# Batch 1 turned in PSUM with its copies apart from TensorE, and a new order on GpSimd, in a fused attention, Fourier mixing and MLP kernel

## The chip, the cores and the metric

The kernel runs on one core of a Trainium2 chip. The metric is the device time of one execution in microseconds (us); the kernel before took 317.34 us (median of three runs, 317.1 to 317.51). The profiled part of an execution, its span, is about 1.8 us shorter than its device time. Engines: PE is TensorE (PEld its weight loads), DVE is VectorE, ACT is ScalarE, POOL is GpSimd, SP is SyncE.

## The reference, cut to what matters

```python
# attention both ways: x (8, 8, 512, 64) with state (8, 8, 32, 64)
scores = x @ state.T / 8;  xread = softmax(scores) @ state      # 512 rows of a batch
scores2 = state @ x.T / 8; sread = softmax(scores2) @ x         # 32 rows of a batch
x = concatenate([xread, sread])          # as (8, 544, 512), float32
# Fourier mixing and an MLP
u  = x + real(fft(fft(x, axis=1), axis=2))
un = (u - mean(u)) / sqrt(var(u) + 1e-6)
out = u + relu(un @ w_ch1) @ w_ch2       # w_ch1 512x2048, w_ch2 2048x512
```

(The softmax and the types are abridged.) Since relu(s·a) = s·relu(a) for a positive s, the kernel multiplies by 1/sqrt(var + 1e-6), its tile `rstd`, only at the very end of a row. This is why `rstd` of batch 0 isn't urgent.

## The kernel before

Eight batches go through one pipeline. While TensorE works on the MLP of one batch, it also gets steps of the next batch's attention and transform. For batches 0 and 1 this overlap is still being built up, and the change is there. The reads of a batch end in tiles XF, XR (rows of the two halves) and XL (32 low rows). They are *folded*, that is, added and subtracted with their mirror images, into XE and XO and then XQ, which the transform multiplies by tables of cosines and sines (`gp`). The results are G, `yp`, U; then `ub` (U minus its mean), turned to `unT`, and the first layer `ph`.

GpSimd works in the order of these lines (cut to what matters):

```python
def more_loads():
    alternate()
    ...
    load_x(2)                                        # SP: x of batch 2
    state_blocks(2, B, nc.gpsimd.tensor_copy)        # casts of states 2 to 7
    nc.gpsimd.tensor_copy(gate, xs_of[2][:, :, 0])   # second gate: reads all four pieces of x
    for q in range(4):
        nc.gpsimd.dma_start(out=w2[...], in_=w2v[...])   # second weights, 4 x 1 MB
    cast_x(2)

def stats_of(u, name):
    ...
    nc.gpsimd.tensor_tensor(rstd, mv[:, 1:2], epst, op=ALU.add)      # a "root": two instructions,
    nc.gpsimd.tensor_tensor(rstd, rstd, mhalf, op=ALU.pow)           # where the statistics are made
    return mv, rstd

def fold_rows(k, eng=nc.vector):
    eng.tensor_add(Sm[:, k], XF[:, k], XR[:, k])
    eng.tensor_add(XE[:, k, 0:256], Sm[:, k, 0:256], Sm[:, k, 512:256:-1])
    eng.tensor_copy(XE[:, k, 256:257], Sm[:, k, 256:257])
    yield
# in batches 0 and 1, GpSimd folds XL and half 0; VectorE folds half 1 and makes XQ
```

A *gate* is a small copy whose only use is to hold GpSimd, and the transfers that it issues next, until its source has landed.

The order of the steps around batch 1 is written out:

```python
for step in (warmed(t0[:2], 2) + [last_sines, more_loads, load_x3] + warmed(t0[2:4], 2) + [exp_again,
        t0[4], t0[8], W(6), s1[1], W(4), t0[5], s1[0], W(16), t0[7], t0[6], s1[2], L[0], s1[3], ...
        L[4], s1[6], t0[13], L[5], L[6], r1[1], r1[2], L[7], r1[3], L[8], r1[4], r1[5], L[9], L[10], r1[7], ...
```

`t0` are steps of batch 0's transform, `L` of its first layer, `s1` and `r1` the scores and reads of batch 1, `W(n)` are n matmuls that only keep TensorE busy. `r1[1]` is sread (with scalings on VectorE), `r1[2]` the low rows' read xlp with GpSimd's low fold.

The softmax here doesn't subtract the row's maximum and nothing guards it: scores larger than these inputs give would overflow.

## Time and profile before

| | before |
|---|---|
| median of three runs | 317.34 us |
| span of the profiled execution | 316.7 us (its device time: 318.47 us) |
| TensorE busy | 298.8 us |
| TensorE idle in the first 100 us | 12.3 us |
| batch 1's transform waits for XQ, then for sT | 1.64 us, 0.86 us |
| x of batch 2 complete, GpSimd's gate opens | 37.82, 38.11 us |

TensorE is full from about 55 us on, so time can only be won ahead of that. The wait for sT is a wait for room: the `gp` tiles and the turned state and x of batch 2 take turns in three PSUM buffers (pool `psQ` in the code), and the third `gp` needs the one out of which VectorE copies batch 2's sT. The lines of the trace stand in the prediction below.

### The profile page before, as it was taken

The page shows a single profiled execution, that of the slowest core. Times are in us where ns is not written, and L with a number is a line of the kernel's source. Part 1 is how long each engine was busy: PE and PEld are TensorE (multiplying, and loading weights), DVE is VectorE, ACT ScalarE, POOL GpSimd, SP SyncE. Part 2 cuts the span into 40 slices and gives each one's busy share as a digit, 9 for nine tenths or more (in the row PEclk, how much of TensorE's full clock was granted, in tenths as well). Part 3 has the DMA queues.
Part 4 walks back from the last instruction along what each step waited for, and adds up shares of the span by engine and source line. Part 5 has one row for each costly group of instructions (what it writes and reads, how often), then busy time and mean ns, then how long its engine had stood idle before and what let it go on. Part 6 is the DMA issues. An engine that isn't in the chain of part 4 may idle for free.

```text
span 316.7 us, 5957 instructions
## 1 busy us (share of the span) xinstructions
PE 298.8 (94%) x2298; PEld 173.0 (55%) x2330; DVE 186.3 (59%) x445; ACT 138.7 (44%) x269; POOL 73.1 (23%) x166
## 2 busy tenths in 40 slices
PE   5878986999999999999999999999999999999995
PEld 5667975554544555456554554455454544455444
DVE  8797565578596684781917864685659573101112
ACT  6698753564553444234442345244433432343300
POOL 8657693240150021300320024001200031000000
PEclk9999999999999999999999999999999999999999
DMA  7998999244836744249363445731342024302055
GB/s 141 197 192 159 203 163 207 62 99 88 165 67 141 174 102 105 81 83 198 77 93 82 69 116 70 147 85 35 83 86 66 35 67 100 83 35 66 35 132 133
DMA packets 111532, 34.22 MB, mean 108 GB/s; under 512 B 102928, under 2 KB 107280, under 8 KB 111504
## 3 DMA queue, kind: packets, MB, share of 16 engines
q1 hardware_dynamic: 100784, 28.08, 43.2%
q0 software_dynamic: 4224, 4.19, 8.4%
q10 hardware_dynamic: 6496, 1.57, 2.4%
q8 instruction: 18, 0.29, 0.4%
q14 instruction: 10, 0.08, 0.1%
HBM read 22.43 MB, written 14.02 MB: 115 GB/s over the span
## 4 chain that ended last, share of the span: by engine, by line
PE 73%; DMA 11%; DVE 9%; POOL 4%; issue 2%; SPq 1%; ACT 0%; POOLq 0%; DVEq 0%
PE po L733 32%; PE ph L667 29%; DMA xs<-in_x_dram 6%; DMA s_dram<-in_state_dram 5%; PE gp L547 3%; DVE U L517 1%; PE po L725 1%; PE yp L513 1%; PE yp L512 1%; DVE st L315 1%; PE eTp L395 1%; PE xfp L408 1%; POOL w L304 1%; DVE ot L698 1%; PE gp L551 1%
## 5 line engine op out<-in xcount | busy, mean ns | idle before, releaser
L733 PE MATMUL po<-w,hT 128*128 128x512 bf16 x477 | 121.9, 379 | 1.4 <-issue 0.8
L669 ACT ACTIVATE hT<-ph 128x512 bf16<-128x512 f32 x112 | 66.9, 597 | 123.5 <-PE ph L667 123.5
L667 PE MATMUL ph<-unT,w 128*128 128x512 bf16 x436 | 114.0, 379 | 1.1 <-DVE ot L698 0.3
L667 PEld LDWEIGHTS <-w 128*128 128x128 bf16 x576 | 51.2, 98 | 48.6 <-issue 1.0
L733 PEld LDWEIGHTS <-hT 128*128 128x128 bf16 x496 | 47.0, 98 | 44.6
L698 DVE SCALAR_TENSOR_TENSOR ot<-po,rstd,U 128x512 f32<-128x512 f32 (+1 forms) x33 | 24.1, 730 | 52.5 <-PE po L733 41.6
L557 POOL COPY GL<-G 128x128 bf16<-128x128 bf16 x8 | 2.4, 300 | 119.6 <-ACT G L555 119.6
L517 DVE TENSOR_TENSOR U<-yp,XR 128x512 f32<-128x512 f32 x16 | 10.9, 682 | 24.4 <-PE yp L513 24.4
L315 DVE BATCH_NORM_STATS2 st<-U 128x6 f32<-128x512 f32 x32 | 21.8, 682 | 0.1
L320 POOL TENSOR_TENSOR rstd<-rstd,mhalf 128x1 f32<-128x1 f32 x34 | 20.3, 597 | 2.7
L319 POOL TENSOR_TENSOR rstd<-mv,epst 128x1 f32<-128x1 f32 x34 | 6.8, 201 | 60.5 <-DVE mv L317 60.5
L555 ACT CAST G<-gp 128x288 bf16<-128x288 f32 x31 | 12.2, 397 | 13.9 <-PE gp L551 8.4
L753 PE MATMUL warm<-ident 128*128 128x128 bf16 x162 | 13.8, 239 | 3.8 <-POOL ident masks.py:199 3.5
L677 PE MATMUL ph<-unT,w 128*128 128x128 bf16 x256 | 15.9, 219 | 0.2 <-ACT unT L591 0.2
L677 PEld LDWEIGHTS <-w 128*128 128x128 bf16 x256 | 15.0, 98 | 0.5 <-issue 0.3
L547 PEld LDWEIGHTS <-XQ 128*128 128x128 bf16 x96 | 8.7, 98 | 11.3 <-DVE XQ L480 4.1
L753 PEld LDWEIGHTS <-ident 128*128 128x128 bf16 x162 | 12.0, 109 | 4.7 <-POOL ident masks.py:199 3.5
L136 POOL CAST xin<-xs 128x2048 bf16<-128x2048 f32 x7 | 13.3, 1895 | 0.0
L581 DVE TENSOR_SCALAR ub<-U,mv 128x512 bf16<-128x512 f32 x24 | 12.3, 513 | 0.9
L408 PEld LDWEIGHTS <-ET 128*128 128x128 bf16 x80 | 7.0, 98 | 10.0 <-DVE XL L417 2.1
L417 DVE TENSOR_TENSOR XR<-xrp,rs 128x512 bf16<-128x512 f32 x16 | 11.1, 695 | 1.2 <-POOL XR L276 0.6
L679 ACT ACTIVATE hT<-ph 128x512 bf16<-128x512 f32 x16 | 9.6, 597 | 5.1 <-PE ph L677 5.1
(183 smaller groups left out, 355.0 us busy)
## 6 DMA issues: line engine op xcount, KB each, us to landing
xs<-in_x_dram SPq DMA_DIRECT2D x30, 256.0 KB, 4.8
w<-in_moe_w_ch_dram POOLq DMA_DIRECT2D x8, 512.0 KB, 11.7
out_dram<-ot SPq DMA_DIRECT2D x15, 256.0 KB, 3.5
r_dram<-ot SPq DMA_DIRECT2D x14, 256.0 KB, 2.2
out_dram<-r_dram SPq DMA_DIRECT2D x14, 256.0 KB, 3.6
xs<-in_x_dram ACTq DMA_DIRECT2D x2, 256.0 KB, 4.1
l_dram<-ot SPq DMA_DIRECT2D x2, 256.0 KB
r_dram<-ot ACTq DMA_DIRECT2D x2, 256.0 KB
```

What stands on the lines that cost most here:

```text
L136: nc.gpsimd.tensor_copy(t[:, :, 1:513], xs)
L315: nc.vector.bn_stats(st6, u)
L320: nc.gpsimd.tensor_tensor(rstd, rstd, mhalf, op=ALU.pow)
L517: nc.vector.tensor_add(u.rearrange("p (k r) -> p k r", r=2), p.rearrange("p (r k) -> p k r", r=2)[:, 0:u.shape[1] // 2, :], x.rearrange("p ...
L547: nc.tensor.matmul(p[:, 0:NM], lhsT=XQ[:, j, c, :], rhs=tab[c], start=(c == 0), stop=(c == 2 and j != 2))
L581: nc.vector.tensor_scalar(t, in0=ud, scalar1=mv[:, 0:1], scalar2=None, op0=ALU.subtract)
L667: nc.tensor.matmul(ph[:, o:o + n], lhsT=w1[:, c, f * 128:(f + 1) * 128], rhs=un_of[key][:, c, :], start=(c == 0), stop=(c == DC - 1))
L669: nc.scalar.activation(hT[:, per * i:per * i + per, :].rearrange("p a b -> p (a b)"), ph, AF.Relu, scale=-1.0 if key in flipped else 1.0)
L677: nc.tensor.matmul(ph[:, o:o + 128], lhsT=w1[:, c, f * 128:(f + 1) * 128], rhs=un_of[key][:, c, 128 * r:128 * r + 128], start=(c == 0), st ...
L698: nc.vector.scalar_tensor_tensor(ot[:, cols], in0=po_of[i][:, 0:cols.stop - cols.start], scalar=rstd, in1=u[:, cols], op0=ALU.mult, op1=AL ...
L733: nc.tensor.matmul(po_of[i], lhsT=h_of[key][:, f, i * 128:(i + 1) * 128], rhs=w2[:, f, :], start=(f == 0), stop=(f == FC - 1))
L753: nc.tensor.matmul(t[:, 0:128], lhsT=ident, rhs=ident, start=(i == 0), stop=(i == n - 1))
```

## The change

The intent has two halves. On GpSimd, the second weights shall be issued as soon as one piece of batch 2's x is there, and the fold of batch 1 shall come ahead of the roots, which nobody needs yet. On TensorE's side, batch 1's x and state are turned into spare PSUM in one go, and the three copies out of it are apart from the turning, so that TensorE doesn't stand behind each copy; sread and xlp change places. Two more edits are not in the cut below: the last two sines of ScalarE come later (after `t0[2:4]`), and `more_loads` is split, its second half (`last_loads`) following them. `weave` interleaves lists of steps; the two numbers behind a list say over which part of the stretch it is spread. The core of the diff:

```diff
-    nc.gpsimd.tensor_copy(gate, xs_of[0][:, :, 0])
+    nc.gpsimd.tensor_copy(gate[:, 0:1], xs_of[0][:, 3, 0:1])
 ...
-        state_blocks(2, B, nc.gpsimd.tensor_copy)
-        nc.gpsimd.tensor_copy(gate, xs_of[2][:, :, 0])
+        nc.gpsimd.tensor_copy(gate[:, 0:1], xs_of[2][:, 0, 0:1])
         for q in range(4):
             nc.gpsimd.dma_start(out=w2[:, q * 4:(q + 1) * 4, :], in_=w2v[:, q * 4:(q + 1) * 4, :])
+        state_blocks(2, 3, nc.gpsimd.tensor_copy)
         cast_x(2)
 ...
+        if roots is None:
+            root()
+        else:
+            roots.append(root)          # batch 0: called after batch 1's fold
 ...
+        def turn_all():
+            p, t = psF.tile([128, 1024], BF16, name="sTp", tag="c"), psX.tile([128, 2, 1024], BF16, name="xTp", tag="x")
+            ...                         # 16 transposes of x, 4 of the state
+            copies.append(lambda: nc.scalar.copy(sT, ...))
+            copies.append(lambda: nc.scalar.copy(xT[:, 0:2, :], t[:, 0]...))
+            copies.append(lambda: nc.vector.tensor_copy(xT[:, 2:4, :], t[:, 1]...))
 ...
-            t0[4], t0[8], W(6), s1[1], W(4), t0[5], s1[0], W(16), t0[7], t0[6], s1[2], L[0], s1[3], ...
-            ... L[5], L[6], r1[1], r1[2], L[7], ... L[9], L[10], r1[7], lambda: state_ones(2, B)]):
+            t0[4], t0[8], W(6), turns1, t0[5], W(10), t0[7], copies1[0], copies1[1], t0[6], copies1[2], L[0], ...
+            r1[2], t0[13], L[5], r1[1], L[6], ... L[8], r1[7],
+            lambda: state_ones(2, B), lambda: [r() for r in first_roots], L[9], L[10]]):
 ...
-          (scores_next, 0.22, 0.86), ([lambda: load_x(4)], 0.6, 0.6))
+          ([lambda: state_blocks(3, B, nc.gpsimd.tensor_copy)], 0.35, 0.35), (scores_next, 0.26, 0.9), ([lambda: load_x(4)], 0.6, 0.6))
```

More of the change, by code (lines that the diff above doesn't have):

```diff
@@ L291, in more_loads @@
     def more_loads():
-        alternate()
         nc.gpsimd.tensor_copy(gate[:, 0:1], XQs[0][:, 3, 0, 0:1])
@@ L296, in more_loads, with last_loads @@
         nc.gpsimd.memset(stb[:, 2:].rearrange("p b g c -> p (b g c)").bitcast(F32), 0.0)
+    def last_loads():
         for hh in range(1, 4):
@@ L311, in x2, with stats_of @@
         return psX.tile([128, 2, 512], F32, name=name, tag="x")
-    def stats_of(u, name):
+    def stats_of(u, name, roots=None):
         st6 = wk.tile([128, 6], F32, name="st6", tag="st6", bufs=4)
@@ L318, in stats_of, with root @@
         rstd = wk.tile([128, 1], F32, name="rstd", tag=name, bufs=16)
-        nc.gpsimd.tensor_tensor(rstd, mv[:, 1:2], epst, op=ALU.add)
-        nc.gpsimd.tensor_tensor(rstd, rstd, mhalf, op=ALU.pow)
+        def root():
+            nc.gpsimd.tensor_tensor(rstd, mv[:, 1:2], epst, op=ALU.add)
+            nc.gpsimd.tensor_tensor(rstd, rstd, mhalf, op=ALU.pow)
+        if roots is None:
+            root()
+        else:
+            roots.append(root)
         return mv, rstd
+    first_roots = []
     x_by_dma, u_by_dma = 3, 2
@@ L347, in turn_state @@
                 return
-            p = psF.tile([128, 1024], BF16, name="sTp", tag="c") if b == 1 else qt("sTp", BF16)
+            p = qt("sTp", BF16)
             for pr in range(4):
@@ L351, in turn_state @@
                 nc.tensor.transpose(p[:, pr * 128:(pr + 1) * 128], sb[:, g, 4 + 128 * hp:132 + 128 * hp], ident)
-            (nc.scalar.copy if b < 2 else nc.vector.tensor_copy)(sT, p[:, 0:512].rearrange("p (a b) -> p a b", b=128))
+            (nc.scalar.copy if b == 0 else nc.vector.tensor_copy)(sT, p[:, 0:512].rearrange("p (a b) -> p a b", b=128))
         def turn_x(g):
@@ L358, in turn_x @@
                 return
-            p = psF.tile([128, 1024], BF16, name="xTp", tag="c") if b == 1 else qt("xTp", BF16)
+            p = qt("xTp", BF16)
             for si in (0, 1, 3, 2):
@@ L363, in turn_x @@
                     nc.tensor.transpose(p[:, o:o + 128], xin[:, si, 1 + 128 * (2 * g + k):129 + 128 * (2 * g + k)], ident)
-            (nc.vector.tensor_copy if b == 0 or g == (b == 1) else nc.scalar.copy)(
+            (nc.vector.tensor_copy if b == 0 or g == 0 else nc.scalar.copy)(
                 xT[:, 2 * g:2 * g + 2, :], p.rearrange("p (a b) -> p a b", b=S))
+        def turn_all():
+            p, t = psF.tile([128, 1024], BF16, name="sTp", tag="c"), psX.tile([128, 2, 1024], BF16, name="xTp", tag="x")
+            for pr in range(4):
+                for si in (0, 1, 3, 2):
+                    nc.tensor.transpose(t[:, pr // 2, 512 * (pr % 2) + 128 * si:512 * (pr % 2) + 128 * si + 128],
+                                        xin[:, si, 1 + 128 * pr:129 + 128 * pr], ident)
+            for pr in range(4):
+                g, hp = pr // 2, pr % 2
+                nc.tensor.transpose(p[:, pr * 128:(pr + 1) * 128], sb[:, g, 4 + 128 * hp:132 + 128 * hp], ident)
+            copies.append(lambda: nc.scalar.copy(sT, p[:, 0:512].rearrange("p (a b) -> p a b", b=128)))
+            copies.append(lambda: nc.scalar.copy(xT[:, 0:2, :], t[:, 0].rearrange("p (a b) -> p a b", b=S)))
+            copies.append(lambda: nc.vector.tensor_copy(xT[:, 2:4, :], t[:, 1].rearrange("p (a b) -> p a b", b=S)))
+        copies = []
         def scores_t(g):
@@ L487, in attend @@
         if b < 2:
-            first = [turn_state, lambda: turn_x(0), lambda: turn_x(1), lambda: scores_t(0), lambda: scores_t(1),
+            first = [turn_state, lambda: turn_x(0), lambda: turn_x(1)]
+            if b == 1:
+                first = [turn_all] + [lambda i=i: copies[i]() for i in range(3)]
+            first += [lambda: scores_t(0), lambda: scores_t(1),
                      lambda: scores(0), lambda: scores(1)]
@@ L572, in centre @@
             u = U[k][:, r, r:r + 512]
-            mv, rstds[k, r] = stats_of(u, "rstd")
+            mv, rstds[k, r] = stats_of(u, "rstd", first_roots if b == 0 else None)
             t = ub[k, r] = wk.tile([128, 512], BF16, name="ub", tag="ub", bufs=5)
@@ L767 @@
     W = lambda n: (lambda: warm(n))
-    for step in (warmed(t0[:2], 2) + [last_sines, more_loads, load_x3] + warmed(t0[2:4], 2) + [exp_again,
-            t0[4], t0[8], W(6), s1[1], W(4), t0[5], s1[0], W(16), t0[7], t0[6], s1[2], L[0], s1[3], t0[9], L[1], t0[10], s1[4],
-            L[2], t0[11], t0[12], L[3], s1[5], r1[0], L[4], s1[6], t0[13], L[5], L[6], r1[1],
-            r1[2], L[7], r1[3], L[8], r1[4], r1[5], L[9], L[10], r1[7], lambda: state_ones(2, B)]):
+    turns1, copies1, s1 = s1[0], s1[1:4], s1[4:]
+    for step in (warmed(t0[:2], 2) + [alternate, more_loads] + warmed(t0[2:4], 2) + [last_sines, exp_again, last_loads, load_x3,
+            t0[4], t0[8], W(6), turns1, t0[5], W(10), t0[7], copies1[0], copies1[1], t0[6], copies1[2],
+            L[0], s1[0], t0[9], L[1], t0[10], s1[1], L[2], t0[11], t0[12], L[3], s1[2], r1[0], L[4], s1[3],
+            r1[2], t0[13], L[5], r1[1], L[6], r1[3], L[7], r1[4], r1[5], L[8], r1[7],
+            lambda: state_ones(2, B), lambda: [r() for r in first_roots], L[9], L[10]]):
         step()
     weave((L[11:], 0, 0.25), (t1, 0.2, 1), ([M[i] for i in (0, 4, 1, 5, 2, 6, 3, 7, 8, 9)], 0.33, 0.99),
-          (scores_next, 0.22, 0.86), ([lambda: load_x(4)], 0.6, 0.6))
+          ([lambda: state_blocks(3, B, nc.gpsimd.tensor_copy)], 0.35, 0.35), (scores_next, 0.26, 0.9), ([lambda: load_x(4)], 0.6, 0.6))
     l2 = M
```

## The prediction

> **What bounds the kernel now.** I read the page first: how full TensorE is and where it is not.
>
> ```profile
> PE 298.8 (94%) x2298; PEld 173.0 (55%) x2330; DVE 186.3 (59%) x445; ACT 138.7 (44%) x269; POOL 73.1 (23%) x166
> ...
> PE   5878986999999999999999999999999999999995
> ```
>
> TensorE is busy 94% of 316.7 us, and from slice 8 on (each slice is 7.9 us) it is full. Whatever the change does must therefore happen in the first seven slices, some 55 us, and a microsecond won there moves everything behind it. Next, busy time by stretch (columns: length, then busy us of PE, PEld, DVE, ACT, POOL):
>
> ```profile
> 20.00:25.00 5.00, 3.43 (x37) 2.49 (x34) 3.67 (x9) 4.97 (x16) 2.07 (x7) 1.00 1.21 197
> 25.00:30.00 5.00, 4.27 (x64) 3.91 (x65) 3.74 (x8) 4.66 (x8) 4.83 (x12) 1.00 0.65 120
> 30.00:40.00 10.00, 10.00 (x169) 9.60 (x167) 6.49 (x18) 7.22 (x14) 5.39 (x8) 1.00 1.10 210
> 40.00:51.40 11.40, 8.57 (x142) 7.97 (x139) 5.55 (x15) 6.61 (x13) 10.21 (x19) 1.00 1.16 172
> 51.40:55.00 3.60, 2.68 (x23) 1.85 (x25) 3.29 (x15) 0.80 (x2) 0.00 (x0) 1.00 1.23 214
> ```
>
> TensorE lacks 1.57 + 0.73 + 0 + 2.83 + 0.92 = 6.05 us there. While it lacks 2.83 us in the fourth stretch, GpSimd is the full engine (10.21 of 11.40). The list of who waited for whom, TensorE from 25 to 60 us (columns: total, times, longest):
>
> ```profile
> PE gp L547 <- DVE XQ L480: 1.6, 1, 1.6
> PE xfp L408 <- DVE XL L417: 1.1, 1, 1.1
> PE gp L547 <- DVE sT L352: 0.9, 1, 0.9
> PE yp L513 <- ACT G L555: 0.6, 1, 0.6
> PE tp L590 <- ACT ub L579: 0.4, 1, 0.4
> PE ph L677 <- ACT unT L591: 0.2, 1, 0.2
> ```
>
> The largest, batch 1's transform (gp) waiting for XQ, leads to VectorE and from there to GpSimd, as the timelines of both show (start, length, instruction, idle before and its end):
>
> ```profile
> 38.11 0.19 POOL L302 COPY gate<-xs 128x4 f32<-128x4 f32 x1 [2.65 <-DMA xs<-in_x_dram]
> 38.57 3.04 POOL L304 DMA_DIRECT2D w<-in_moe_w_ch_dram  x4 [0.27 <-issue]
> 41.58 1.93 POOL L136 CAST xin<-xs 128x2048 bf16<-128x2048 f32 x1
> 43.41 0.33 POOL L557 COPY GL<-G 128x128 bf16<-128x128 bf16 x1
> ...
> 47.22 0.67 POOL L462 TENSOR_TENSOR XE<-XL 32x256 f32<-32x256 bf16 x1
> ...
> 50.57 0.19 POOL L471 CAST XE<-Sm 128x1 f32<-128x1 bf16 x1
> ```
>
> ```profile
> 50.79 0.56 DVE L480 TENSOR_TENSOR XQ<-XE 128x384 bf16<-128x384 f32 x1 [3.53 <-POOL XE L471]
> ```
>
> VectorE had its own half of the fold by 47.3 us and then stood 3.53 us until GpSimd's half came at 50.76. GpSimd was late because it works in order: it waited for all of batch 2's x (37.8), spent 3.04 us issuing the second weights, 1.93 on a cast, 0.33 on GL, and 3.5 us (43.67 to 47.14) on four pairs of rstd, which nobody needs before the first output at 63.96 us. Only then came the folds, 3.5 us.
>
> **What the Trainium skill says.** "Perfetto Trace Analysis", section "Tensor Engine Instruction (MATMUL, LD_WEIGHTS)": ACT, DVE and GpSimd are strict first in, first out. The trace agrees: folds whose XL was there at 41.4 us stand behind roots until 47.2. "DMA: Bandwidth & Descriptors", section "Queues, rings and completion order": each DMA engine goes round robin between queues, a packet at a time. The trace agrees: packet by packet, the SP queue (256-byte packets) moved 221 KB/us from 29 to 36 us alone, but 40 KB/us from 17 to 25 us beside the first weights, which moved 155. "SBUF — State Buffer", section "SBUF: two separate sides": GpSimd and VectorE share a port pair that one instruction holds whole. The trace fits: VectorE's Sm over 128x514 took 0.66 us beside batch 0's GpSimd fold, 0.43 us in batch 1 where GpSimd did a root.
>
> **The change, part by part.** The built order of both kernels was compared engine by engine.
>
> *First gate.* The copy ahead of the first weights now reads one piece of x. The copy before it ends at 10.1 us, when all of x of batch 0 (last piece 8.3) has landed. Worth 0.
>
> *Second gate and GpSimd's order.* It waits for the second piece of batch 2's x, which landed at 34.04 us (all: 37.82). The weights issue at about 34.4 to 37.5. Then the state casts of batch 2 alone: the four of 768 elements took 3.73 us; I take 1.0 us for 128 elements each, so 38.5. The cast of x, if x is in by then: 40.4. The low fold, 1.45 us (0.67 + 0.14 + 0.63): 41.9. Sm needs XF and XR, which I put at 40.6 below: 43.1; XE 0.8: 43.9. So GpSimd's half comes at about 44 instead of 50.8, ahead of TensorE. Roots move to 44 to 47.5, the casts of the other states later; both are needed only from 60 us on.
>
> *ScalarE's order in the head.* The copy of G (j=2) no longer stands behind two sines (23.89 to 24.66): it starts at 23.9, and the yp that waited 0.55 us is held only by VectorE's G of 24.84. So U starts at 25.28 instead of 25.72, and mv is ready at 26.92. ub no longer waits behind the 1.0 us copy of xT: it starts at 26.95, not 27.78. With the old distances (0.78 to tp, 0.43 to unT, 0.64 to ph) ph starts at 28.75 instead of 29.63. But ScalarE now has unT, sT (0.49) and xT (0.91) in a row: xT is there at 30.0, scores start at 30.05 (before 30.52), TensorE idles 0.4 us, and the next ub comes at 30.65, another 0.2 us. By the xrp of batch 1 (34.90 before) I expect 34.65. Of 0.9 us won, 0.25 stays. The ten warm matmuls fewer (10 at about 56 ns) only fill a wait: 0.
>
> *xlp ahead of sread.* Before, xfp stood 1.06 us behind XL, plus 0.16 once more. Now xlp comes one step of the first layer and one score after xrp, so XL is early (37.4). XF is then behind sread's four scalings (1.17 us) on VectorE: I work out waits of 0.3 before the second xfp and 0.3 before the last xrp. Net 1.2 - 0.6 = 0.6 us. The last xrp now precedes two more steps of the first layer (0.89 us each), so VectorE's fold is done at 43.3, XQ begins at 44 and is complete at 47. TensorE, after seven steps, reaches gp at 48.5 to 48.9 and finds XQ: the 1.64 us fall away.
>
> *sT.* The 0.86 us stood behind VectorE's six XQ passes and eight memsets (50.8 to 54.2). These are now done before TensorE arrives, so the copy follows its transpose: 0.86 us fall away.
>
> Sum: 0.25 + 0.6 + 1.64 + 0.86 = 3.35 us, perhaps 0.3 more from the small waits. Taken: 3.6 us, so 317.34 - 3.6 = 313.7. From 55 us on TensorE is full and does the same work, so the shift is kept.
>
> **Rivals.**
>
> *The second weights hold up x.* Issued at 34.4, their packets start about 1.9 us later (before: 38.57 to 40.46), at 36.3, when batch 2's last small piece and all of batch 3's x are under way. Slowed by 221/40 = 5.5, the remaining 1.5 us would take 8.3: x at 44.6, cast 46.5, folds 50: the 1.64 us stay, and with part of the 0.86 the gain is 1 to 1.5, time about 316. For it: the rates above. Against it: at 36.5 all of the piece before it and six of the small piece's eight writes had landed, and batch 3's last small piece met the start of the same weights and took 1.46 us after its predecessor, against 1.34. XQ has about 4 us to spare.
>
> *VectorE becomes the bound at 60 to 80 us* (16.8 of 20 busy). TensorE lacks only 0.94 us there now, and VectorE's work there hangs on TensorE's own products, so it moves with them. If it eats the gain: 315.5. The changed weave (scores of batch 2 a little later) can move this by 0.5 either way.
>
> *ScalarE's row of copies costs more than it saves.* If the scores wait longer than 0.4 us, up to 0.7 goes: 314.4.
>
> *All idle time goes*: 6.05 us at most, 311.3. The waits inside batch 0's fold (before 23 us) are untouched, so this is unlikely.
>
> **Range and chances.** Between the first rival and the best case, leaning to the sum: 312.4 to 315.6. Two per cent are 6.3 us, more than all idle time in reach: faster 0.04, same 0.95, slower 0.01.
>
> **What would show it.** GpSimd's last XE at 43 to 46 us, ahead of gp. No wait of gp for XQ or sT over 0.3 us. The weights issued at 34.4. A cast of batch 2's x starting by 41; beyond 44 the first rival is right. First ph at 28.7, then a wait of the scores for xT. gp of batch 1 at 48.5 to 49 and, from yp on, all of TensorE's work 3.3 to 3.9 us earlier to the end. Wrong if gp still waits, or if the gain at 55 us is not there at 311.

## The result, and the profile after

The changed kernel took 315.34 us (median of four runs, 315.33 to 315.38) against 317.22 (four runs, 317.09 to 317.51) for the kernel before. The ratio is 0.994, 95% interval 0.9922 to 0.9957. A ratio here is the mean time of one kernel's fast runs over that of the other's of the same rounds, so it isn't quite the ratio of the medians quoted. Executions over 1.5% slower than the fastest of the same kernel are left out of the means. The spans of the two traces are 316.7 and 313.6 us: trace to trace the gain is 3.1 us, timed it is 1.9.

The page of the changed kernel, busy time of each engine and TensorE in 40 slices:

```profile
PE 300.5 (96%) x2320; PEld 172.4 (55%) x2320; DVE 187.0 (60%) x445; ACT 138.5 (44%) x269; POOL 74.8 (24%) x170
...
PE   5878999999999999999999999999999999999995
```

The 8, 7 and 6 in slices 5 to 7 have become 9. Busy time by stretch, as in the prediction (length, then busy us of PE, PEld, DVE, ACT, POOL, granted clock, DMA, GB/s):

```profile
20.00:25.00 5.00, 3.75 (x39) 2.72 (x37) 3.53 (x9) 4.96 (x16) 2.04 (x6) 1.00 1.21 197
25.00:30.00 5.00, 4.03 (x61) 3.48 (x59) 3.17 (x7) 4.12 (x7) 4.86 (x13) 1.00 0.46 80
40.00:51.40 11.40, 11.13 (x168) 9.96 (x166) 7.77 (x23) 7.47 (x17) 10.71 (x18) 1.00 1.19 189
51.40:55.00 3.60, 3.60 (x32) 2.30 (x30) 0.88 (x2) 1.73 (x3) 1.63 (x3) 1.00 1.18 234
```

TensorE now lacks 0.27 us from 40 to 51.4 us, where it lacked 2.83, and nothing from 51.4 to 55, where it lacked 0.92. GpSimd is just as full from 40 to 51.4, and TensorE no longer minds. TensorE's waits from 25 to 60 us (total, times, longest):

```profile
PE ph L706 <- ACT unT L620: 0.7, 1, 0.7
PE eTp L398 <- ACT xT L388: 0.4, 1, 0.4
```

The waits for XQ, sT, XL, G and ub are gone. The wait of the first ph for unT was there before too (0.23 us); that it is 0.67 now I put down to the ten fewer matmuls that do nothing ahead of it, which wasn't tested (ph itself starts at 28.65, earlier than the 29.63 of before). GpSimd's timeline (start, length, instruction, idle before it and what ended that):

```profile
35.17 0.19 POOL L302 COPY gate<-xs 128x1 f32<-128x1 f32 x1 [4.57 <-DMA xs<-in_x_dram]
35.63 3.04 POOL L304 DMA_DIRECT2D w<-in_moe_w_ch_dram  x4 [0.28 <-issue]
...
40.05 1.89 POOL L136 CAST xin<-xs 128x2048 bf16<-128x2048 f32 x1
42.03 0.66 POOL L488 TENSOR_TENSOR XE<-XL 32x256 f32<-32x256 bf16 x1
...
45.68 0.18 POOL L497 CAST XE<-Sm 128x1 f32<-128x1 bf16 x1
45.81 0.19 POOL L322 TENSOR_TENSOR rstd<-mv,epst 128x1 f32<-128x1 f32 x1
```

The fold's last piece ends at 45.86 instead of 50.76, and the roots follow it. VectorE and TensorE then:

```profile
45.90 0.56 DVE L506 TENSOR_TENSOR XQ<-XE 128x384 bf16<-128x384 f32 x1 [0.63 <-POOL XE L497]
```

```profile
48.56 0.41 PE L576 MATMUL gp<-CT,XQ 128*128 128x288 bf16 x2
...
61.60 0.38 PE L619 MATMUL tp<-ident,ub 128*128 128x128 bf16 x4 [0.63 <-ACT ET L422]
```

VectorE now waits 0.63 us for GpSimd instead of 3.53, and XQ is complete at 48.66, hardly ahead of use: `gp` takes its parts one after another from 48.56. Behind it, `yp` starts at 54.10 instead of 58.04. Of these 3.94 us the last line gives some back: at 61.6 us TensorE waits 0.63 us for ScalarE's ET, a wait that the kernel before doesn't have. At the end of the span 3.1 us are left.

### The profile page after: what moved, and what is told of

Same layout as the page of the kernel before. It is cut to its first block, busy times and chain, and to the rows that moved or that the text cites. A ratio compares the mean times of both kernels' runs of the same rounds, so it can differ in the third digit from the quotient of the medians.

```text
span 313.6 us, 5980 instructions
## 1 busy us (share of the span) xinstructions
PE 300.5 (96%) x2320; PEld 172.4 (55%) x2320; DVE 187.0 (60%) x445; ACT 138.5 (44%) x269; POOL 74.8 (24%) x170
## 4 chain that ended last, share of the span: by engine, by line
PE 81%; DVE 12%; ACT 2%; DMA 2%; issue 1%; SPq 0%; DVEq 0%; ACTq 0%
PE po L762 32%; PE ph L696 29%; PE gp L576 3%; PE ph L706 3%; DMA xs<-in_x_dram 2%; DVE U L546 2%; DVE st L316 1%; PE yp L542 1%; PE po L754 1%; PE yp L541 1%; PE xfp L434 1%; PE xrp L434 1%; PE gp L580 1%; PE esp L409 1%; DVE XF L443 1%
## 5 line engine op out<-in xcount | busy, mean ns | idle before, releaser
L762 PE MATMUL po<-w,hT 128*128 128x512 bf16 x496 | 125.0, 379 | 0.0
L782 PE MATMUL warm<-ident 128*128 128x128 bf16 x152 | 12.8, 237 | 3.8 <-POOL ident masks.py:199 3.4
L782 PEld LDWEIGHTS <-ident 128*128 128x128 bf16 x152 | 11.1, 107 | 4.7 <-POOL ident masks.py:199 3.4
```

What stands on the lines that cost most here:

```text
L762: nc.tensor.matmul(po_of[i], lhsT=h_of[key][:, f, i * 128:(i + 1) * 128], rhs=w2[:, f, :], start=(f == 0), stop=(f == FC - 1))
L782: nc.tensor.matmul(t[:, 0:128], lhsT=ident, rhs=ident, start=(i == 0), stop=(i == n - 1))
```

## The experiments

All ran on one chip and gave correct results. The runs of the kernel before: 318.43 us (316.55 to 319.61, 11 runs), 316.65 (316.37 to 316.93, 7 runs). The second call has 318.44 (12 runs), but 11 of these are those of the first, so the ratios of e5 to e8 rest on runs of the kernel before from another call. Already these medians tell something: the kernel before moves over 3.2 us, the changed one stays within 315.33 to 315.44 in the ten runs that there are.

Theory A: the wait of 1.64 us isn't a constant of the kernel before. It follows when batch 2's x lands, and was large in the one execution that was traced. Theory B: the predicted gain was there and was lost again later in the changed kernel.

### The kernel before, four traces (before, e1, e9, e12)

No edit. First run:

> The kernel before, unchanged, for a second trace of it. Why: the trace that the prediction was read from belongs to an execution of 318.47 us, while the timed executions took 317.1 to 317.5, so some 1.2 us of what I counted may be peculiar to that execution. Theory A (the last small piece of batch 2's x lands at a time that varies, and the kernel before passes that on through GpSimd to gp): span near 315.4, the gate of the second weights opens before 37.5 us instead of 38.11, and the wait of gp for XQ in batch 1 is 0.4 to 0.8 us instead of 1.6. Theory B (the extra time of that execution lies elsewhere): the wait for XQ is again about 1.6 and another wait or a longer instruction accounts for 1.2 us.

It took 318.05 us (317.13 to 319.68, four runs; ratio 0.999, 0.9953 to 1.0028). The traced execution fell on the slow end, 319.68 us, span 317.9, so the expected small wait missed; a larger one was seen. TensorE's and GpSimd's lines of it:

```profile
52.60 0.42 PE L547 MATMUL gp<-CT,XQ 128*128 128x288 bf16 x2 [2.89 <-DVE XQ L480]
```

```profile
39.10 0.19 POOL L302 COPY gate<-xs 128x4 f32<-128x4 f32 x1 [2.82 <-DMA xs<-in_x_dram]
```

Two more were taken:

> The kernel before once more, for a third trace. Two traces so far: gate of the second weights 38.11, wait of gp for XQ 1.64, span 316.7; gate 39.10, wait 2.9, span 317.9. Theory A says span minus wait is constant (315.1 and 315.0) and the wait follows the gate: here again the span is 315.0 plus that wait, within 0.2 us, wherever the gate falls. If the span moves without the wait, theory A falls.

> The kernel before, a fourth trace, with the same expectation as for the third: span minus the wait of gp for XQ (batch 1) is 315.0 within 0.2 us.

The first gave 316.38 us (both are single runs, at a granted clock of 1.00), and no wait for XQ at all, with a shorter one for sT:

```profile
49.52 0.41 PE L547 MATMUL gp<-CT,XQ 128*128 128x288 bf16 x2
...
52.62 0.41 PE L547 MATMUL gp<-ST,XQ 128*128 128x288 bf16 x2 [0.49 <-DVE sT L352]
```

The second gave 317.27 us. All four, in order of the gate:

| trace of before | x of batch 2 in | gate opens | GpSimd's last XE starts | wait for XQ | wait for sT | span | span less both waits |
|---|---|---|---|---|---|---|---|
| e9 | 35.68 | 35.97 | 48.43 | 0 | 0.49 | 314.6 | 314.1 |
| e12 | 36.59 | 36.88 | 49.36 | 0.50 | 0.86 | 315.5 | 314.1 |
| before | 37.82 | 38.11 | 50.57 | 1.64 | 0.86 | 316.7 | 314.2 |
| e1 | 38.81 | 39.10 | 51.77 | 2.89 | 0.86 | 317.9 | 314.2 |

The last column is constant. The gate opens 0.29 us behind x, GpSimd's last XE starts 12.5 to 12.7 us behind the gate, and TensorE comes to `gp` at 49.5 to 49.8 in each (start less wait): what pushes XQ past that costs time one for one. Theory A is shown, by these four traces and by e2, e10 and e11 below, which change GpSimd alone. My expectation for e9 had counted the wait for XQ alone and so was 0.4 off; that for e12 held. SP issues x of batch 2 only when the copy of the state rows ahead of it has landed (at 26.55, 27.28, 27.64 and 28.76, same order; x is issued at 27.19, 27.92, 28.27 and 29.40), so the spread comes from there; why that copy varies stays open. Not all of the spread need be this wait: two of the 11 runs (319.50 and 319.61) have a mean granted clock of 0.995, the others 0.998 to 1.000, and neither was traced.

### GpSimd's part alone, on the kernel before (e2)

```diff
-        state_blocks(2, B, nc.gpsimd.tensor_copy)
-        nc.gpsimd.tensor_copy(gate, xs_of[2][:, :, 0])
+        nc.gpsimd.tensor_copy(gate[:, 0:1], xs_of[2][:, 0, 0:1])
         for q in range(4): ...
+        state_blocks(2, 3, nc.gpsimd.tensor_copy)
 ...                                   # roots of batch 0 after batch 1's fold, states 3 to 7 later
```

The first gate is changed here too. The other engines' orders are those of before.

> The kernel before with only the GpSimd part of the change: weights by the second piece of x, casts of batch 2's state alone, fold ahead of the roots. TensorE, VectorE and ScalarE keep the order of before. Theory A (GpSimd's late fold is the main loss): gp no longer waits for XQ beyond VectorE's own fold (which ends at 47.3), and the 0.9 us for sT shrink too: 1.5 to 2.5 us faster than before in one trace against another, 0.3 to 1.5 in the timed runs if before's first trace was slow by 1.2. Rival (the turning and copies carry the gain): under 0.3 us in the timed runs.

It took 315.82 us (315.70 to 315.94, six runs), ratio 0.9916 (0.9889 to 0.9942), span 313.9. Batch 1's waits for XQ and sT are gone; the wait of 1.1 us of xfp for XL is still there. Against the same runs of before (318.43), GpSimd's part brings 2.6 of the 3.0 us that the changed kernel (e5) gains, and the steadiness as well.

### The changed kernel without GpSimd's part (e3)

The reverse of the above, on the changed kernel: second gate on all of x, casts of all states ahead of it (and no longer in the weave), roots at once. The first gate stays changed.

```diff
-        nc.gpsimd.tensor_copy(gate[:, 0:1], xs_of[2][:, 0, 0:1])
+        state_blocks(2, B, nc.gpsimd.tensor_copy)
+        nc.gpsimd.tensor_copy(gate, xs_of[2][:, :, 0])
 ...
-            mv, rstds[k, r] = stats_of(u, "rstd", first_roots if b == 0 else None)
+            mv, rstds[k, r] = stats_of(u, "rstd")
```

> The changed kernel with the GpSimd order of before (all casts of state and all of x ahead of the weights, roots ahead of the fold); TensorE, VectorE and ScalarE in the order of the change. Theory A: TensorE reaches gp at about 48.6 and then waits some 2.5 us for XQ, so nearly all of the gain is lost: within 0.5 us of before. Rival: it keeps more than half of the 1.9 us.

It took 320.27 us (319.16 to 321.88, six runs), ratio 1.006 (1.0028 to 1.0092): slower than before, by 1.8 us where at most 0.5 was expected. TensorE's own half of the change brings it to `gp` sooner, at 48.68, where it stands until GpSimd is done:

```profile
52.00 0.66 PE L576 MATMUL gp<-CT,XQ 128*128 128x288 bf16 x2 [3.32 <-DVE XQ L506]
```

and then the granted clock (the third number from the end in these stretches) is halved:

```profile
49.00:50.00 1.00, 0.00 (x0) 0.00 (x0) 0.00 (x0) 0.32 (x1) 0.92 (x2) 1.00 1.21 192
50.00:51.00 1.00, 0.00 (x0) 0.00 (x0) 0.00 (x0) 0.00 (x0) 0.92 (x2) 0.89 1.22 194
51.00:52.00 1.00, 0.00 (x1) 0.01 (x1) 0.62 (x2) 0.00 (x0) 0.35 (x2) 0.50 1.21 194
...
57.00:58.00 1.00, 1.00 (x11) 0.88 (x10) 0.07 (x1) 0.40 (x1) 0.00 (x0) 0.70 0.95 190
```

A mean of 0.89 in the second line means that it fell at about 50.8, and 0.70 in the last that it rose at about 57.6 (both worked out from two levels, 1 and 0.5). "TensorE: Matmul & The Clock Gate", section "Part 1: The HAM clock gate (the "warmup" mystery)" of the Trainium skill has this: half the clock after an idle window of about 3.4 us, and windows that run free of the program. The trace agrees in kind, though not in the length: 0.50 after some 2.1 us of idleness, and the 2.89 us of e1 passed with 1.00 throughout. The span fits: 313.6 + 3.32 of waiting = 316.9, measured 319.5; the 2.6 us left are about half of the 5.6 us that TensorE ran from 52.0 to 57.6 at half the clock. The timed runs say the same: the mean granted clock is 0.989 in two (321.26 and 321.88 us), 0.994 to 0.995 in three (319.85 to 320.57) and 0.999 in the last (319.16). That last one lies within the range of the kernel before, so what the kernel loses beyond before is, as far as six runs show, the clock's.

### The weave of before in the changed kernel (e4)

```diff
-          ... (scores_next, 0.26, 0.9), ...
+          ... (scores_next, 0.22, 0.86), ...
```

> The changed kernel with the scores of batch 2 woven in at the old place (0.22 to 0.86 instead of 0.26 to 0.9). In the changed kernel a transpose of u waits 0.63 us at 61 us for ScalarE's ET, a wait that the kernel before had not. Theory: the later weave made it; here it is gone and the time falls by 0.3 to 0.6 us. Rival: the transposes and copies of batch 2's x now stand earlier and hold up gp by as much, so the time stays within 0.2 us of the changed kernel's 315.34.

315.0 us (314.95 to 315.02, six runs), ratio 0.9889 (0.9865 to 0.9913), span 313.2. The wait for ET isn't in its trace; the later wait of 0.3 us of batch 2's `gp` for XQ (at about 75 us) is in both kernels. So the new weave cost 0.4 us of the change's gain: theory B is true for that much, and no more.

### The changed kernel again (e5)

> The changed kernel unchanged, on the chip of this call, so that the others can be set against it: 315.0 to 315.5, spread under 0.3 us, while the kernel before spreads over 1 us or more on the same chip. If the changed kernel spreads as widely, theory A (the kernel before passes the late landing of x on, the changed one has slack for it) falls.

315.41 us (315.33 to 315.44, six runs), ratio 0.9901 (0.9875 to 0.9928), span 313.6. The same two kernels gave a ratio of 0.994 at first; the difference is that of the kernel before.

### Roots at once, all else changed (e6)

```diff
-            mv, rstds[k, r] = stats_of(u, "rstd", first_roots if b == 0 else None)
+            mv, rstds[k, r] = stats_of(u, "rstd")
```

> The changed kernel with the four pairs of roots of batch 0 ahead of the fold again, all else as changed (weights still by the second piece). The pairs took 3.3 to 3.9 us on GpSimd. In the changed kernel the fold ended at 45.9 and gp began at 48.6, so the fold now ends near 49.3 and XQ is there at 49.8. Theory (the order of roots and fold is worth what it puts beyond TensorE's arrival): gp waits 0.7 to 1.5 us for XQ, the time is 0.7 to 1.8 us above the changed kernel. Rival (the gate of the weights is what matters, the roots had room): within 0.2 us.

317.45 us (317.04 to 319.03, six runs), ratio 0.9972 (0.9944 to 1.0), span 315.6. New waits of TensorE from 25 to 60 us (the second is for batch 2's sT, as in the kernel before):

```profile
PE gp L576 <- DVE XQ L510: 0.8, 1, 0.8
PE xTp L373 <- DVE sT L362: 0.7, 1, 0.7
...
PE gp L576 <- DVE XQ L507: 0.2, 1, 0.2
```

Although the gate opened at 33.44 in this trace, the four pairs of roots stood from 40.27 to 43.5 and the fold ended at 47.46. In the changed kernel, where TensorE comes about 1.2 us sooner than before, the order of the roots is worth 2.0 us (317.45 less 315.41), a little more than expected. The fold's delay is not all of it. With the roots gone from behind the fold, GpSimd's casts of the other states follow it at once, beside VectorE's passes over XQ, three of which took 0.96 to 1.07 us instead of 0.56:

```profile
47.38 3.89 POOL L155 CAST stb<-gen 32x640 bf16<-32x640 f32 x4
47.49 1.03 DVE L506 TENSOR_TENSOR XQ<-XE 128x384 bf16<-128x384 f32 x1 [2.76 <-POOL XE L497]
```

The fold ended 1.6 us later than in the changed kernel, but XQ was complete 3.5 us later (52.16 against 48.66). How the 2.0 us divide between the two wasn't tested.

### No second gate (e7)

```diff
-        nc.gpsimd.tensor_copy(gate[:, 0:1], xs_of[2][:, 0, 0:1])
```

> The changed kernel with the second weights issued as soon as the first have landed, without waiting for any of batch 2's x: issue at about 30.6 instead of 35.6. Theory (my first rival of the prediction, made strong on purpose): the weights take four fifths of the DMA packets' time from 33 us on, x's last pieces land at 41 us or later, GpSimd's cast waits for them, the fold ends after 48 and gp waits for XQ: 0.5 to 4 us slower than the changed kernel. Rival (the gate is not needed, x comes in time): within 0.3 us of it.

320.58 us (318.0 to 325.48, six runs), ratio of its fast runs 1.0026 (0.9978 to 1.0075). The four fast runs (318.0 to 322.12) are 2.6 to 6.7 us above e5. The traced run was a slow one, 325.26, so its lengths aren't compared; but it shows where the cast of x stood:

```profile
49.62 1.89 POOL L136 CAST xin<-xs 128x2048 bf16<-128x2048 f32 x1 [14.66 <-DMA xs<-in_x_dram]
```

The weights were issued at 30.49 and x's last piece landed at 49.30 instead of 37.97. This is the first rival of the prediction, brought about on purpose. A gate is needed; waiting for one piece of x was enough.

### VectorE takes both copies of xT, weave of before (e8)

```diff
-            copies.append(lambda: nc.scalar.copy(xT[:, 0:2, :], ...))
+            copies.append(lambda: nc.vector.tensor_copy(xT[:, 0:2, :], ...))
 ...
-          ... (scores_next, 0.26, 0.9), ...
+          ... (scores_next, 0.22, 0.86), ...
```

In the changed kernel VectorE's half of xT stood 1.56 us behind ScalarE's half (both read one PSUM tile and write one SBUF tile; which of the two makes the wait wasn't tested):

```profile
30.03 0.69 DVE L389 COPY xT<-xTp 128x1024 bf16<-128x1024 bf16 x1 [1.56 <-ACT xT L388]
```

> The changed kernel with both halves of batch 1's xT copied by VectorE (in the changed kernel VectorE stood idle 1.56 us at 28.5 to 30.0 because its half waited for ScalarE's) and with the scores of batch 2 woven in at the old place. Theory: the scores no longer wait 0.35 us for ScalarE's copy, the second ub starts at 29.1 instead of 29.9, so 0.4 to 0.8 us are won at the first layer and about 0.3 by the weave: 314.2 to 314.7, faster than both kernels. Rival: VectorE's copies push back its own U and the fold, or the microseconds go into the wait for XQ, and the time stays at 315.0.

314.83 us (314.79 to 314.87, six runs), ratio 0.9884 (0.986 to 0.9908), span 313.0: the best of all, ahead of both kernels. VectorE's copies:

```profile
26.82 0.69 DVE L388 COPY xT<-xTp 128x1024 bf16<-128x1024 bf16 x1
...
29.17 0.66 DVE L389 COPY xT<-xTp 128x1024 bf16<-128x1024 bf16 x1
```

They fit into VectorE's idle time, and the scores' wait for xT is gone. ScalarE, relieved of 1.03 us, has the second ub at 29.28 instead of 29.88. Against e4, this is 0.17 us, less than the 0.4 to 0.8 expected of the copies. It was run at another time.

### One GpSimd step at a time, on the kernel before (e10, e11)

The gate alone (e10):

```diff
-        nc.gpsimd.tensor_copy(gate, xs_of[2][:, :, 0])
+        nc.gpsimd.tensor_copy(gate[:, 0:1], xs_of[2][:, 0, 0:1])
```

> The kernel before with one line changed: the second weights wait for the second piece of batch 2's x, not for all of it. Everything else on GpSimd stays, roots ahead of the fold. The weights issue some 2 to 3 us earlier, but the cast behind them still waits for all of x, so GpSimd gains the 3.04 us of issuing only as far as it fits before x has landed: the fold ends 2 to 3 us earlier, near 48 to 49 us, XQ is there at about 48.5 to 49.5, and TensorE arrives at 49.8: the wait for XQ goes, part of the 0.9 us for sT stays. Span 314.3 to 314.9, time 316.0 to 316.7. Rival (x is held up by the weights, as without a gate): the wait stays over 1 us.

315.75 us (315.71 to 315.89, four runs), ratio 0.9973 (0.9958 to 0.9988), span 314.1; better than I expected. The gate opened at 34.65, and GpSimd's last XE started at 46.55.

The roots alone (e11), that is, the `roots` list and its call after batch 1's fold, nothing else:

> The kernel before with only the roots of batch 0 moved behind batch 1's fold. GpSimd's fold comes 3.3 to 3.5 us earlier, so it ends at 46.5 to 48.5 instead of 50 to 52, and the wait of gp for XQ goes to between 0 and 0.3 us; the wait for sT goes too where the fold ends before 48. Time 315.6 to 316.3, as good as the whole GpSimd part (315.82). Rival (the second gate is needed as well): over 316.6.

315.87 us (315.86 to 315.90, four runs), ratio 0.9976 (0.9959 to 0.9992), span 314.1, as expected. The gate opened at 37.13, and still the fold was done at 46.36:

```profile
46.18 0.18 POOL L480 CAST XE<-Sm 128x1 f32<-128x1 bf16 x1
46.32 0.45 POOL L321 TENSOR_TENSOR rstd<-mv,epst 128x1 f32<-128x1 f32 x1
```

Neither trace has a wait of batch 1 for XQ or sT, though x came early in both (36.65 and 36.83). Both come to the span that the table of before gives without its waits, 314.1. Each step takes the fold out of the way by itself, and the second has nothing left to win on the kernel before. That this holds for the latest x too wasn't traced; all eight timed runs stay within 315.71 to 315.90.

## Why the prediction was right or wrong

The time was 1.6 us too low, and only 0.26 us were left to the upper end of the range. That the range held is in part luck: two steps were off, both in the same direction. The mechanism, a fold that came too late and TensorE waiting for it, was as predicted. The term that was mis-sized is "the 1.64 us fall away", and the step that failed is "the shift is kept".

- **XQ.** It did fall away. But 1.64 was the wait of one execution of 318.47 us, and I took it off a median of 317.34. In four traces the wait was 0, 0.50, 1.64 and 2.89 us. The median of 317.22 of the rounds of the result answers to a span of about 315.45, so to waits for XQ and sT of 315.45 - 314.1 = 1.35 us together, not 2.5 (an estimate from the table). From the traced execution's own time the same sum gives 318.47 - 3.6 = 314.9, 0.5 off.
- **sT.** It fell away with XQ, as reasoned. It too is 0.49 where GpSimd is early enough.
- **Second gate.** The piece landed later than in the trace of before, and the gate opened at 35.17, not 34.1; the casts of the states took 1.37, not 1.0. The fold came at 45.9, not 43.9, within the 43 to 46 given. In e5 the gate opened at 34.68: these times shift between executions too.
- **Head.** ph at 28.65 (28.75 predicted), the scores' wait 0.35 (0.4), xrp at 34.62 (34.65). The VectorE copy's wait of 1.56 was not foreseen; e8, which takes it away, wins 0.17 on e4.
- **xlp ahead of sread.** The two waits of 0.3 that I allowed for VectorE's scalings aren't in the list. TensorE came to gp at 48.56 against 49.77 (51.41 less 1.64), 1.2 us sooner instead of 0.85 with both parts of the head. Turning and this exchange were not tested apart.
- **Kept to the end?** No. Of 3.94 us at yp, 3.1 are left at the end, where the prediction's own sign of being wrong was a gain at 55 us that isn't there at 311. The changed weave, which I gave 0.5 us either way, made the new wait for ET of 0.63; e4 shows 0.4 us for it. So of TensorE's half some 0.4 to 0.5 us is left (e2 315.82 against e5 315.41; spans of 313.9 to 314.1 against 313.6).

Added up for a median execution: 1.35 from the waits and 0.5 from the head, 1.85, against 1.88 measured. In the traced execution: 2.5 and 0.5, 3.0, against 3.1.

The rivals: the second weights didn't hold up x (last piece 37.97; 44.6 predicted for the rival), and only e7, without any gate, shows what they can do. VectorE is no bound at 60 to 80 us (13.8 of 20 busy; TensorE's new wait there is for ScalarE). ScalarE's row of copies cost 0.35 us at the scores. The first gate was taken as worth 0 and wasn't tested by itself; nothing in the traces asks for more.

## What to carry to other kernels

A trace shows one execution: set its time beside the timed ones before taking a wait out of it off the median, and look at what the wait hangs on, above all if it is a transfer. A step that removes a wait which varies makes the kernel steadier as well as faster, and two such steps on one chain don't add up. Speeding up the engine that waits, while what it waits for stays late, can cost time twice, by the wait and by the clock that falls in it.

## What the Trainium skill lacked or had wrong

- "TensorE: Matmul & The Clock Gate", Part 1: the idle window of about 3.4 us isn't a threshold for a gap. In e3 TensorE idled 3.32 us, from 48.68, and the granted clock fell at about 50.8, some 2.1 us into the gap, so the window that ended there can't have been idle throughout; how idle it must be the page doesn't say. In e7 it fell about 2.2 us into a gap of 7.09 us (at 50.9, from a mean of 0.59 over 50 to 55); in e1 a gap of 2.89 us left it at 1.00. A gap under 3.4 us can so be hit or missed. The return at about 57.6 is no contradiction: it is 6.8 us behind the fall, about two of the page's windows, though only 5.6 us behind the first matmul.
- "SBUF — State Buffer", section "SBUF: two separate sides": it says that the loser of the shared ports blocks. The page has the loser slower, but doesn't say outright how a profile shows it: as length of the instruction, not as a wait. VectorE's XE of 128x256 took 1.27 us at 43.94 beside GpSimd's Sm (43.53, 1.40 us), and 0.43 us in the kernel before.
- "DMA: Bandwidth & Descriptors", section "Queues, rings and completion order": the round robin by packets is there, not what follows from it. With both queues full, from 17 to 25 us of the kernel before, each moved 155 packets per us, as the profile counts them (a packet of the page holds several descriptors); at 1,024 and 256 bytes that is 155 and 40 KB/us, while the small packets alone made 221. The share went by packet size.
- No page tells how far the landing of one load moves between executions of one kernel: x of batch 2 was complete at 35.68 to 38.81 us in four traces, and the time of these four moved by 3.3 us with it.
